# The first chunk's first layer in two halves of its contraction, one more weight piece split on TensorE and ScalarE, and a new order of the first steps

## The chip, the core and the metric

The kernel runs on one core of a Trainium2 chip. The metric is the device time of one execution in microseconds (us), lower is better. A core has five engines that each work through their own instructions in order and wait for each other through semaphores: TensorE (PE in the profile; its weight loads are listed apart as PEld), VectorE (DVE), ScalarE (ACT), GpSimd (POOL) and SyncE (SP), which here only issues DMAs.

## What is computed

Attention with a band of 16 keys to either side and one summary key and value per block of 32 (4 batches, 8 heads, 768 positions, 64 dimensions), and behind it a two-layer network with a GELU on the 3072 resulting rows of 512. Cut to what matters:

```
k_sum = k.reshape(B, H, nb, 32, D).max(axis=3)
v_sum = v.reshape(B, H, nb, 32, D).mean(axis=3)
scores_l = where(|i - j| < 16, scale * q @ k.T, -1e9)
scores_s = scale * q @ k_sum.T + log(32)
a = softmax(concat([scores_l, scores_s]))
x = (a @ concat([v, v_sum]))          # regrouped to (3072, 512)
h = x @ w_in                          # w_in: 512 x 2048
g = 0.5 * h * (1 + erf(h / sqrt(2)))
out = g @ w_out                       # w_out: 2048 x 512
```

All inputs are float32. TensorE takes float16 here, so a large product is made of three: each operand a is split into a high half (a rounded to float16) and a low half (the rest), and high x high, high x low and low x high are summed. A few early products are made in float32 instead.

## The kernel before

**Attention units.** The attention runs in 24 units of 4 heads x 256 positions; the first six lie in batch 0. Units 0 to 2 work in float32 (`f_scores`, `f_sums`, `f_values`), later ones with halves (`scores`, `sums`, `values`). A unit's path: `k_pack` (ACT packs keys and block maxima into `kf`), `f_mask` (PE writes the mask into PSUM), `f_scores` (PE), `evac` (ACT), `maximum` (POOL, a maximum over partitions), `m_shift` (PE subtracts it), `m_exponent` (ACT), `f_sums` and `f_values` (PE), `norm_take`, `norm_cross`, `norm_rec`, `norm_spread`, `norm_mult` (DVE, but `norm_cross` is ACT's), and `x_hi` (ACT) and `x_lo` (DVE), which leave the rows of x as two halves in `xos`. `f_values` needs the means of the summary values in its value tile; `s_load_vs` (ACT) or `load_vs` (POOL) copies them from the result of `sum_vt` (PE) and `mean_vt` (ACT).

**The network.** A chunk is 256 rows of x; chunk c takes units 2c and 2c+1, one for each half of the contraction over 512. `phase1 c i` multiplies it with piece i of `w_in` (8 pieces of 256 columns) in 24 products of 128x256: for each of two output halves e, four contraction blocks k, three products each. Blocks k = 0, 1 come from the first unit and k = 2, 3 from the second. `gelu`, `g_hi` (ACT) and `g_lo` (DVE) follow, and `phase2` multiplies with `w_out`. From chunk 4 on another scheme is used, which the change doesn't touch.

**Weights.** The weights arrive as 64-bit floats. `fetch_w_in` loads a piece, three DVE passes (`wi_bits i 0, 1, 2`) turn the bits into float32 in `wt`, `wi_hi` (ACT) makes the high half in `ww`, and the low half comes in one of two ways. `wi_lo` is one DVE pass. `wi_diff i h` and `wi_dlo i h` do half a piece each: PE takes wt minus the high half with a scaled identity (`eye`, float32) and its negative (`neg`, float16), and ACT writes the result as float16:

```
def wi_diff(i, h):
    ps = diffs["i", i, h] = ps_h.tile([P, 2, CH], F32, tag="psh", name=f"psw_{i}_{h}")
    ...
    nc.tensor.matmul(flat, eye, wt[:, i, h * 512 : (h + 1) * 512], start=True, stop=False)
    nc.tensor.matmul(flat, neg, w_part(i, 0, ks), start=False, stop=True)
...
def wi_dlo(i, h):
    ...
    nc.scalar.activation(w_part(i, 1, ks), flat.rearrange("p (r j) -> p r j", j=P), AF.Copy)
```

Before the change, piece 5 alone is done in the second way.

**Order.** `ORDER` is a table of 1936 steps. The program goes through it once, and each step appends its instructions to its engines, so the table sets the order on every engine and of the DMAs on SP's queue. `SLOTS` says which buffer each tile of a pool takes. Steps that start with `a_` issue their DMA from ACT's queue.

**Fills.** `fill n` is a step in which PE multiplies ones by ones into a PSUM tile that nobody reads: 3 products of 512 columns into `pso`, or 6 of 256 into `psd`. There are nine, and 16 such products of 512 columns at the very start (`pso_fill_s`). Each of the two PSUM pools has one buffer.

Of the kernel before, what the change touches and what calls it, by code (L numbers as in the profile page):

```python
# [84 lines left out]
wi_bits 4 2, wi_bits 5 0, sum_vt 1, evac 2, norm_take 0, wi_hi 4, wi_bits 5 1, fill 0, norm_cross 0, sum_vt 2, load_q
3, m_shift 1, s_q_hi 3, wi_bits 5 2, mean_vt, s_load_vs 0, maximum 2, m_shift 2, k_sums 0 0, fetch_w_in 2 2, norm_rec
0, load_v 1, f_values 0, norm_spread 0, wi_lo 4, fetch_w_in 3 3, q_lo 3, wi_bits 2 0, wi_bits 2 1, load_v 2, norm_mult
0, m_exponent 1, wi_bits 2 2, load_q 4, s_load_vs 1, load_k 4, x_hi 0, m_exponent 2, x_lo 0, f_sums 1, norm_take 1,
f_values 1, wi_bits 3 0, wi_bits 3 1, f_mask 3, norm_cross 1, scores 3, evac 3, wi_hi 5, fetch_w_in 1 1, fill 2,
load_v 4, norm_rec 1, norm_spread 1, wi_bits 3 2, norm_mult 1, s_k_hi 4, x_hi 1, fill 3, f_sums 2, norm_take 2,  # L90
load_vs 2, f_mask 4, wi_hi 3, s_q_hi 4, x_lo 1, norm_cross 2, k_lo 4, wi_diff 5 0, wi_dlo 5 0, wi_diff 5 1, f_values
2, phase1 0 4, maximum 3, fetch_k 1 3, load_v 3, wi_bits 1 0, load_vs 3, q_lo 4, wi_bits 1 1, shift 3, wi_bits 1 2,
phase1 0 0, wi_hi 2, load_vs 4, norm_rec 2, norm_spread 2, exponent 3, wi_dlo 5 1, wi_lo 3, phase1 0 5, wi_hi 1,
norm_mult 2, gelu 0 4, gelu 0 5, prep_k 1 3, wi_lo 2, fetch_w_in 6 2, f_sums 3, norm_take 3, x_hi 2, wi_lo 1, scores
4, load_k 5, wi_bits 6 0, fetch_k 1 0, norm_cross 3, f_values 3, norm_rec 3, x_lo 2, evac 4, maximum 4, fetch_w_in 7
3, norm_spread 3, prep_k 1 0, phase1 0 3, phase1 0 1, gelu 0 0, g_hi 0 4, norm_mult 3, load_q 5, wi_bits 6 1, s_q_hi
5, x_hi 3, q_lo 5, phase1 0 2, g_hi 0 0, fetch_w_out 0 4, fetch_w_out 1 5, gelu 0 3, fetch_k 2 1, x_lo 3, shift 4,
g_hi 0 5, wi_bits 6 2, s_k_hi 5, k_lo 5, g_lo 0 4, g_lo 0 5, exponent 4, wo_bits 0 0, gelu 0 1, phase1 1 4, f_values
4, wi_bits 7 0, g_lo 0 0, load_k 6, wo_bits 0 1, g_hi 0 3, gelu 0 2, s_k_hi 6, f_sums 4, norm_take 4, wo_bits 0 2,
gelu 1 4, wi_bits 7 1, load_q 6, load_v 5, wi_hi 6, phase1 1 3, g_hi 0 2, wo_bits 1 0, g_hi 0 1, g_lo 0 1, wo_hi 0,  # L100
phase1 1 1, norm_cross 4, wo_bits 1 1, wi_bits 7 2, fetch_w_out 2 4, phase1 1 0, wo_lo 0, g_hi 1 4, gelu 1 1, g_lo 0
3, wi_hi 7, fetch_k 1 1, f_mask 5, scores 5, evac 5, phase1 1 5, wo_bits 1 2, g_lo 1 4, wo_hi 1, wi_lo 7, gelu 1 3,
g_hi 1 1, wi_lo 6, s_q_hi 6, g_hi 1 3, q_lo 6, gelu 1 5, g_hi 1 5, wo_lo 1, g_lo 1 5, prep_k 1 1, f_mask 6, phase1 1
2, prep_k 2 1, gelu 1 2, fetch_w_out 3 5, maximum 5, phase1 0 7, phase1 0 6, wo_bits 2 0, g_lo 1 3, wo_bits 2 1,
norm_rec 4, norm_spread 4, wo_bits 2 2, g_lo 0 2, wo_bits 3 0, gelu 0 7, prep_k_end 1 0, wo_bits 3 1, gelu 1 0, phase1
1 6, k_sums 1 0, g_hi 1 0, load_v 6, g_hi 1 2, g_lo 1 1, wo_bits 3 2, phase2 0 1, gelu 0 6, g_lo 1 2, shift 5,
fetch_w_out 4 4, k_lo 6, wo_hi 3, load_q 7, wo_hi 2, wo_lo 2, exponent 5, wo_lo 3, g_hi 0 6, wo_bits 4 0, norm_mult 4,
phase2 0 0, s_q_hi 7, wo_bits 4 1, phase1 1 7, gelu 1 7, scores 6, load_vs 5, fetch_w_out 5 5, x_hi 4, wo_bits 5 0,
wo_bits 4 2, f_sums 5, f_values 5, wo_bits 5 1, norm_take 5, evac 6, phase2 0 2, wo_bits 5 2, f_mask 7, g_hi 0 7,
wo_hi 4, wo_lo 4, norm_cross 5, fetch_v 1 2, wo_hi 5, wo_lo 5, phase2 0 3, norm_rec 5, norm_spread 5, x_lo 4,  # L110
norm_mult 5, g_lo 1 0, maximum 6, load_v 7, x_hi 5, x_lo 5, q_lo 7, fetch_w_out 6 4, g_lo 0 7, phase2 0 5, g_hi 1 7,
shift 6, fetch_k 1 2, phase2 0 4, gelu 1 6, load_k 7, s_k_hi 7, wo_bits 6 0, phase1 2 6, gelu 2 6, exponent 6, k_lo 7,
fetch_w_out 7 5, prep_v 1 2, g_lo 0 6, g_lo 1 7, phase1 2 4, gelu 2 4, load_k 9, wo_bits 7 0, g_hi 1 6, prep_k 1 2,
prep_k_end 1 1, g_hi 2 4, g_lo 1 6, phase1 2 1, wo_bits 7 1, s_p_hi 6, wo_bits 6 1, wo_bits 7 2, phase1 2 0, gelu 2 1,
fetch_v 1 1, load_q 9, p_lo 6, gelu 2 0, fetch_v 1 0, load_mask, k_sums 1 1, wo_hi 7, s_q_hi 9, wo_bits 6 2, phase1 2
7, wo_hi 6, wo_lo 7, wo_lo 6, scores 7, s_k_hi 9, sums 6, fetch_v 1 3, prep_v 1 1, q_lo 9, prep_v 1 0, fetch_k 2 0,
fetch_v 2 1, prep_v 1 3, phase1 2 3, k_lo 9, fetch_k 2 3, load_vs 6, phase2 0 6, store 0 0, phase2 0 7, g_hi 2 1, g_lo
2 1, g_lo 2 4, norm_take 6, evac 7, load_q 8, prep_k 2 0, prep_v 2 1, phase2 1 0, g_hi 2 6, phase2 1 2, phase2 1 4,
gelu 2 3, gelu 2 7, prep_k 2 3, norm_cross 6, load_vs 7, v_hi 6, maximum 7, load_k 8, wt_add 1 0, g_hi 2 7, v_hi 7,
s_k_hi 8, wt_add 1 1, v_lo 6, fetch_v 2 2, shift 7, s_q_hi 8, v_lo 7, exponent 7, norm_rec 6, scores 9, values 6,  # L120
load_v 9, prep_k_end 2 0, phase2 1 6, k_lo 8, q_lo 8, norm_spread 6, load_k 11, g_hi 2 3, prep_v 2 2, add_mask 9,
s_p_hi 7, p_lo 7, load_q 11, maximum 9, norm_mult 6, wt_add 1 2, x_hi 6, phase1 2 5, g_lo 2 6, phase1 2 2, put 0 0,
wt_hi 1, store 1 0, s_q_hi 11, scores 8, x_lo 6, gelu 2 5, add_mask 8, load_v 8, sums 7, norm_take 7, load_vs 9,
norm_cross 7, put 1 0, wt_lo 1, g_lo 2 7, fetch_k 2 2, shift 9, s_k_hi 11, norm_rec 7, q_lo 11, maximum 8, gelu 2 2,
values 7, g_hi 2 2, v_hi 9, phase2 1 1, norm_spread 7, phase2 1 3, store 0 1, g_hi 2 5, norm_mult 7, k_lo 11, x_hi 7,
g_hi 2 0, g_lo 2 2, x_lo 7, phase2 1 5, shift 8, exponent 8, v_lo 9, phase1 3 2, prep_k 2 2, g_lo 2 5, s_p_hi 8,
phase2 1 7, load_q 10, p_lo 8, s_q_hi 10, wt_add 0 0, g_lo 2 0, load_vs 8, v_hi 8, exponent 9, load_k 10, fetch_v 2 0,
v_lo 8, load_v 11, phase1 3 4, s_k_hi 10, sums 8, g_lo 2 3, scores 11, add_mask 11, load_v 10, wt_add 0 1, values 8,
put 0 1, q_lo 10, wt_add 0 2, phase1 3 5, gelu 3 2, load_vs 10, k_lo 10, norm_take 8, s_p_hi 9, p_lo 9, phase1 3 6,
maximum 11, wt_hi 0, norm_cross 8, sums 9, scores 10, norm_rec 8, norm_spread 8, q_cast 12, load_k 12, gelu 3 6, store  # L130
1 1, norm_mult 8, gelu 3 5, prep_v 2 0, load_vs 11, x_hi 8, add_mask 10, v_hi 10, values 9, norm_take 9, wt_lo 0, ws
0, norm_cross 9, g_hi 3 6, put 1 1, shift 11, g_hi 3 2, gelu 3 4, x_lo 8, fetch_v 2 3, exponent 11, phase1 3 1,
norm_rec 9, norm_spread 9, s_p_hi 11, norm_mult 9, maximum 10, q_neg 12, v_hi 11, k_sums 2 0, phase1 3 7, v_lo 10,
phase2 2 1, g_lo 3 2, phase2 2 3, shift 10, phase1 3 0, wt_add 2 0, v_lo 11, load_v 12, exponent 10, g_hi 3 5, p_lo
# [1409 lines left out]
```

## Time and profile before

| | us |
|---|---|
| median of three runs | 560.56 |
| the three runs | 559.53, 560.56, 561.64 |
| the profiled execution: its own time | 559.72 |
| its span, from the first instruction to the last | 557.7 |
| busy in the span: PE / PEld | 551.1 / 415.9 |
| busy in the span: DVE / ACT / POOL | 480.2 / 387.8 / 110.8 |

An engine is busy while one of its instructions runs; with PE, products overlap, so its busy time says how long at least one was under way. The difference between the profiled execution's time and its span, 2.0 us, lies before the first and behind the last instruction.

### The profile page before, as it was taken

To read this page: it belongs to the slowest core of one execution; us is meant where nothing else is said; L and a number is where in the kernel's file an instruction comes from. 1 tells how busy PE (TensorE), PEld (TensorE's weight loads), DVE (VectorE), ACT (ScalarE), POOL (GpSimd) and SP (SyncE) were. 2 spreads that over 40 slices of the span, in tenths; PEclk is the share of its full clock that TensorE was granted. 3 is DMA by queue.
4 is the path that set the end of the run, shared out by engine and by line. 5 is a ranking of instruction groups with operands and counts; after the bars stand their busy time and mean duration, and the time that the engine had idled before them with its cause. 6 is when DMAs were issued, how large, how long until landed. Compare 5 with 4: busy or idle time off the path is not lost.

```text
span 557.7 us, 14490 instructions
## 1 busy us (share of the span) xinstructions
PE 551.1 (99%) x6161; PEld 415.9 (75%) x6161; DVE 480.2 (86%) x679; ACT 387.8 (70%) x678; POOL 110.8 (20%) x66
## 2 busy tenths in 40 slices
PE   8999999999999999999999999999999999999997
PEld 5558886685677566677765657888888888888886
DVE  5899999999989999999999989998887895384811
ACT  4698858568688988689887568686577765355610
POOL 2644030302415223163312202103220000000000
PEclk9999999999999999999999999999999999999999
DMA  8979535757455656636565442447954220000102
GB/s 327 398 278 396 212 126 177 263 145 208 157 168 171 138 140 192 141 53 179 138 155 154 151 123 81 104 138 197 286 177 148 61 94 1 1 1 29 48 1 86
DMA packets 42640, 84.26 MB, mean 151 GB/s; under 512 B 4176, under 2 KB 16720, under 8 KB 42064
## 3 DMA queue, kind: packets, MB, share of 16 engines
q1 hardware_dynamic: 38832, 79.85, 43.3%
q0 software_dynamic: 3456, 3.15, 5.1%
q8 instruction: 48, 0.79, 0.6%
q10 hardware_dynamic: 288, 0.34, 0.2%
q14 instruction: 16, 0.13, 0.1%
...
## 4 chain that ended last, share of the span: by engine, by line
PE 97%; ACT 1%; POOL 1%; issue 0%; POOLq 0%
PE psy L1105 15%; PE pso_y L1389 8%; PE pso L1153 8%; PE psz L1105 8%; PE pso L1154 7%; PE pso L1155 7%; PE psh L1034 5%; PE psh L1035 5%; PE psh L1036 5%; PE psx L1105 4%; PE psd_y L1389 4%; PE pss_x L1389 4%; PE pss L875 3%; PE psv L957 3%; PE psv_z L1389 2%; PE psn L973 1%
## 5 line engine op out<-in xcount | busy, mean ns | idle before, releaser
L904 POOL PARTITION_ALL_REDUCE m<-s x23 | 82.0, 3566 | 185.8 <-DVE w_out_l L589 40.8
L1105 PEld LDWEIGHTS <-wt 128*128 128x128 f16 x768 | 74.4, 98 | 10.1 <-issue 0.2
L1153 PE MATMUL pso<-w_out_h,gg 128*128 128x512 f16 x192 | 72.9, 380 | 0.0
L1154 PE MATMUL pso<-w_out_l,gg 128*128 128x512 f16 x192 | 72.8, 379 | 0.0
L1155 PE MATMUL pso<-w_out_h,gg 128*128 128x512 f16 x192 | 72.8, 379 | 0.0
L1105 PE MATMUL psy<-xos,wt 128*128 128x256 f16 x576 | 70.5, 273 | 0.0
L1034 PE MATMUL psh<-xos,ww 128*128 128x256 f16 x256 | 69.9, 273 | 0.0
L1036 PE MATMUL psh<-xos,ww 128*128 128x256 f16 x256 | 69.8, 273 | 0.0
L1035 PE MATMUL psh<-xos,ww 128*128 128x256 f16 x256 | 69.8, 273 | 0.0
L1105 PEld LDWEIGHTS <-ww 128*128 128x128 f16 x576 | 55.8, 98 | 8.9 <-issue 0.4
L1389 PEld LDWEIGHTS <-gg 128*128 128x128 f16 x576 | 55.9, 98 | 7.6 <-issue 1.1
L1116 ACT ACTIVATE ww<-psy 128x512 f32<-128x512 f32 x48 | 28.3, 591 | 27.4 <-PE psy L1105 27.3
L1155 PEld LDWEIGHTS <-gg 128*128 128x128 f16 x192 | 18.8, 98 | 22.7
L1153 PEld LDWEIGHTS <-gg 128*128 128x128 f16 x192 | 18.8, 98 | 19.8 <-issue 0.4
L1154 PEld LDWEIGHTS <-gg 128*128 128x128 f16 x192 | 18.8, 98 | 19.1
L1389 PEld LDWEIGHTS <-wt 128*128 128x128 f16 x288 | 28.1, 98 | 3.6 <-issue 0.4
L1232 DVE SCALAR_TENSOR_TENSOR gg<-h,gg 128x512 f16<-128x512 f32 x32 | 21.5, 686 | 10.1 <-ACT gg L1229 9.9
L1034 PEld LDWEIGHTS <-ww 128*128 128x128 f16 x256 | 25.0, 98 | 4.5 <-issue 0.8
L1035 PEld LDWEIGHTS <-ww 128*128 128x128 f16 x256 | 25.1, 98 | 3.5
L1036 PEld LDWEIGHTS <-ww 128*128 128x128 f16 x256 | 25.1, 98 | 2.9
L1043 ACT ACTIVATE g<-psh 128x512 f32<-128x512 f32 x32 | 19.0, 593 | 10.9 <-DVE gg L1052 6.7
L909 DVE TENSOR_TENSOR s<-s,m 128x1024 f32<-128x1024 f32 x21 | 25.6, 1217 | 0.1
(224 smaller groups left out, 1372.3 us busy)
## 6 DMA issues: line engine op xcount, KB each, us to landing
...
```

Source lines behind the costliest of these rows:

```text
L904: nc.gpsimd.partition_all_reduce(out_ap=self.m32, in_ap=self.s32, channels=P, reduce_op=bass_isa.ReduceOp.max)
L909: nc.vector.tensor_tensor(out=self.s32, in0=self.s32, in1=self.m32, op=ALU.subtract)
L1034: nc.tensor.matmul(ph[:, e, :], wh, xh, start=(k == 0), stop=False)
L1035: nc.tensor.matmul(ph[:, e, :], wh, xl, start=False, stop=False)
L1036: nc.tensor.matmul(ph[:, e, :], wl, xh, start=False, stop=(k == NCC - 1))
L1105: nc.tensor.matmul(ps[:, e, :], ws, xx, start=(first and e == 0 and k == 0 and m == 0), stop=(k == 1 and m == 2), skip_group_check=True,)
L1116: nc.scalar.activation(snaps[b, q, n], split8(acc[b, q, "y"]), AF.Copy)
L1153: nc.tensor.matmul(p, gh, w_out_h[:, f, :], start=(f == 0), stop=False)
L1154: nc.tensor.matmul(p, gh, w_out_l[:, f, :], start=False, stop=False)
L1155: nc.tensor.matmul(p, gl, w_out_h[:, f, :], start=False, stop=(f == NFC - 1))
L1232: nc.vector.scalar_tensor_tensor(out=a_part(b, q, m, 1), in0=h_src(b, q, m), scalar=SC_G, in1=a_part(b, q, m, 0), op0=ALU.mult, op1=ALU.su ...
L1389: nc.tensor.matmul(ps, g, ww_, start=(first and e == 0 and k == 0), stop=(e == 1 and k == 2), skip_group_check=True,)
```

## The change

`phase1` takes a third argument. Without it all 24 products are issued as before; with h = 0 or 1, only the 12 of one half of the contraction: h = 0 needs the first unit of the chunk alone, h = 1 the second. The two halves add up in the same PSUM tile, for which the first product of the tile alone now carries the start flag. All eight pieces of chunk 0 are issued in halves; for pieces 0 and 4 other steps stand between the two halves, for the other six the halves follow each other directly.

Piece 3's low half is no longer made by `wi_lo` but by `wi_diff 3 h` and `wi_dlo 3 h`, as piece 5's is.

The first 419 steps of `ORDER` become 430 in a new order; they are the same steps but for those two changes. The 1517 steps behind them are unchanged, and from there on each tile follows the same tile in its buffer as before. `SLOTS` is rewritten to go with it.

```diff
@@ ORDER (its first two lines; some 80 more are re-sorted)
-fill 10, a_load_m16, fetch_k 0 0, a_load_q 0, fill 8, fetch_w_in 0 0, prep_k 0 0, k_pack 0, prep_k_end 0 0, fill 1,
-f_mask 0, fetch_k 0 1, load_ind, f_scores 0, fetch_vt 0, fill 12, fetch_w_in 4 4, wi_bits 0 0, load_q 1, evac 0,
...
+a_load_q 0, fetch_k 0 0, prep_k 0 0, a_load_m16, fetch_w_in 0 0, fill 3, wi_bits 0 0, wi_bits 0 1, f_mask 0, fill 2,
+fetch_k 0 1, load_ind, wi_bits 0 2, k_pack 0, f_scores 0, k_pack 2, evac 0, fill 4, prep_k 0 1, fill 12, fetch_vt 0,
...
-    def phase1(c, i):
-        ph = pht[c, i] = ps_h.tile([P, 2, CH], F32, tag="psh", name=f"psh_{c}_{i}")
+    def phase1(c, i, h=None):
+        if not h:
+            pht[c, i] = ps_h.tile([P, 2, CH], F32, tag="psh", name=f"psh_{c}_{i}")
+        ph = pht[c, i]
+        ks = range(NCC) if h is None else range(2 * h, 2 * h + 2)
         for e in range(2):
-            for k in range(NCC):
+            for k in ks:
                 x = xo[2 * c + k // 2]
                 wh, wl = (ww[:, z, k, e, i, :] for z in range(2))
                 xh, xl = (x[:, z, k % 2, :] for z in range(2))
-                nc.tensor.matmul(ph[:, e, :], wh, xh, start=(k == 0), stop=False)
-                nc.tensor.matmul(ph[:, e, :], wh, xl, start=False, stop=False)
-                nc.tensor.matmul(ph[:, e, :], wl, xh, start=False, stop=(k == NCC - 1))
+                for m, (ws, xx) in enumerate(((wh, xh), (wh, xl), (wl, xh))):
+                    nc.tensor.matmul(
+                        ph[:, e, :], ws, xx, start=(e == 0 and k == 0 and m == 0),
+                        stop=(k == NCC - 1 and m == 2), skip_group_check=True,
+                    )
```

Three places show what the new order does. The first is PE's, from unit 0's scores (`pss_0`) to its `m_shift` (the row that reads `m32_0`); `psv_vt` is `sum_vt`, and each fill stands here with one row of its three or six. Before:

```order
L796 MATMUL pss_0_157<-q32_0_136,kf_0_147 128x64 x16
...
L442 MATMUL pso_fill_12_181<-ones_89 64x512
...
L442 MATMUL psd_fill_11_194<-ones_89 64x256
...
L651 MATMUL psv_vt_212<-w_out_h_97,w_out_l_98 88x512 x2
...
L764 MATMUL pss_1_0_215<-mask16_sb_88 128x2x64
...
L855 MATMUL pss_0_157<-m32_0_207,neg_1_87 128x512 x2
```

And of the change:

```order
L797 MATMUL pss_0_145<-q32_0_130,kf_0_157 128x64 x16
...
L443 MATMUL pso_fill_4_181<-ones_89 64x512
...
L443 MATMUL pso_fill_12_186<-ones_89 64x512
...
L765 MATMUL pss_1_0_201<-mask16_sb_88 128x2x64
...
L443 MATMUL psd_fill_11_217<-ones_89 64x256
...
L443 MATMUL psd_fill_0_224<-ones_89 64x256
...
L652 MATMUL psv_vt_231<-w_out_h_97,w_out_l_98 88x512 x2
...
L443 MATMUL psd_fill_8_234<-ones_89 64x256
...
L856 MATMUL pss_0_145<-m32_0_211,neg_1_87 128x512 x2
```

Unit 1's mask and two more fills have moved ahead of `m_shift`, one of them and the mask ahead of `sum_vt` too; ahead of the scores stand two fills in place of three.

The second place is PE's too, where the first layer begins. `psn` is `f_sums`, `psv_1` and `psv_2` are `f_values`, `psw` is `wi_diff`, `psh_0_4` is `phase1 0 4`; of 12 or 24 like products one row stands. Before:

```order
L818 MATMUL psn_2_476<-wt_94,ones_f_92 32x256 x4
...
L537 MATMUL psw_5_0_500<-wt_94,w_out_l_98 128x512
...
L537 MATMUL psw_5_1_504<-wt_94,w_out_l_98 128x512
...
L810 MATMUL psv_2_507<-wt_94,v32_2_356 64x64 x16
...
L1034 MATMUL psh_0_4_524<-xos_96,ww_93 128x256
...
L1034 MATMUL psh_0_0_562<-xos_96,ww_93 128x256
```

And of the change:

```order
L819 MATMUL psn_2_449<-wt_94,ones_f_92 32x256 x4
...
L1039 MATMUL psh_0_0_465<-xos_96,ww_93 128x256
...
L811 MATMUL psv_1_479<-s32_1_265,v32_1_351 64x64 x16
...
L1039 MATMUL psh_0_4_500<-xos_96,ww_93 128x256
...
L538 MATMUL psw_3_1_523<-wt_94,w_out_l_98 128x512
L539 LDWEIGHTS w_out_l_98
L539 MATMUL psw_3_1_523<-ww_93,w_out_l_98 128x512
L811 MATMUL psv_2_539<-wt_94,v32_2_375 64x64 x16
...
L538 MATMUL psw_3_0_558<-wt_94,w_out_l_98 128x512
```

The first halves of pieces 0 and 4 now stand ahead of the values of units 1 and 2, and piece 3's two differences between those; piece 5's have moved further ahead. Further on, and not shown here, the first product of the second layer (`phase2 0 0`) now stands behind eleven pieces of the first layer (six of chunk 0, five of chunk 1), where before it stood behind fifteen.

The third place is ACT's, from unit 2's `evac` (the row that writes `wt` from `pss_2`) to `s_load_vs 0` (the row that writes `v32_0`). `rc_0` is `norm_cross 0`, `qh_3` is `s_q_hi 3`, `w_out_h` from `psv_vt` is `mean_vt`, and `s32_1` from `pss_1` is `m_exponent 1`. Before:

```order
L891 ACTIVATE wt_94<-pss_2_246 128x1024
L526 ACTIVATE ww_93<-wt_94 128x8x128
L988 ACTIVATE rc_0_305<-dent_0_294 128x16
L993 ACTIVATE rc_0_305<-dent_0_294 32x8 x4
L829 ACTIVATE qh_3_317<-q32_3_313 128x512
L658 ACTIVATE w_out_h_97<-psv_vt_212 24x512
L723 ACTIVATE v32_0_283<-w_out_h_97 24x1024
```

And of the change:

```order
L892 ACTIVATE wt_94<-pss_2_279 128x1024
L989 ACTIVATE rc_0_304<-dent_0_299 128x16
L994 ACTIVATE rc_0_304<-dent_0_299 32x8 x4
L527 ACTIVATE ww_93<-wt_94 128x8x128 x2
L659 ACTIVATE w_out_h_97<-psv_vt_231 24x512
L863 ACTIVATE s32_1_265<-pss_1_0_201 128x512
L863 ACTIVATE s32_1_265<-pss_1_1_202 128x512
L724 ACTIVATE v32_0_322<-w_out_h_97 24x1024
```

`s_load_vs 0` now stands behind two `wi_hi` and behind `m_exponent 1`, and `s_q_hi 3` has moved behind it.

## Rows read from the trace of the kernel before

**Rows 1.** The page: PE's busy time, and the granted clock in 40 slices.
```profile
PE 551.1 (99%) x6161; PEld 415.9 (75%) x6161; DVE 480.2 (86%) x679; ACT 387.8 (70%) x678; POOL 110.8 (20%) x66
...
PEclk9999999999999999999999999999999999999999
```

**Rows 2.** Waits of PE: what for, total us, times, longest us.
```profile
PE pso_fill_s L442 <- POOL warm L454: 0.9, 1, 0.9
PE psv_vt L651 <- DMA w_out_h<-in_vt_dram: 0.7, 1, 0.7
PE pso_y L1389 <- ACT g_os L1411: 0.5, 1, 0.5
PE psv L810 <- ACT v L723: 0.5, 1, 0.5
PE pss L764 <- ACT wt L862: 0.4, 1, 0.4
PE pss L855 <- POOL m L904: 0.3, 1, 0.3
```

**Rows 3.** Windows: stretch, busy us (instructions) of PE, PEld, DVE, ACT, POOL.
```profile
40.00:60.00 20.00, 20.00 (x252) 17.46 (x249) 19.97 (x27) 16.63 (x29) 6.59 (x3) 1.00 0.81 309
...
400.00:500.00 100.00, 100.00 (x1087) 88.06 (x1086) 75.93 (x116) 64.60 (x124) 3.22 (x1) 1.00 0.25 80
```

**Rows 4.** Timeline of PE: start us, us, instruction, idle before it and its releaser.
```profile
0.94 5.07 PE L442 MATMUL pso_fill_s<-ones 128*64 128x512 f16 x16 [0.94 <-POOL warm L454]
6.07 0.81 PE L442 MATMUL pso_fill<-ones 128*64 128x512 f16 x3
6.72 0.82 PE L442 MATMUL psd_fill<-ones 128*64 128x256 f16 x6
...
8.65 2.00 PE L796 MATMUL pss<-q,kf 64*128 64x64 f32 x32
...
12.79 1.92 PE L651 MATMUL psv_vt<-w_out_h,w_out_l 128*88 128x512 f32 x4 [0.71 <-DMA w_out_h<-in_vt_dram]
14.55 0.60 PE L764 MATMUL pss<-mask_sb 128*128 128x128 f16 x4
...
28.45 1.15 PE L810 MATMUL psv<-s,v 128*64 128x64 f32 x32
...
36.65 1.08 PE L537 MATMUL psw<-wt,w_out_l 128*128 128x512 f32 x2
...
38.95 1.15 PE L810 MATMUL psv<-wt,v 128*64 128x64 f32 x32
...
40.15 0.27 PE L1035 MATMUL psh<-xos,ww 128*128 128x256 f16 x1
40.26 0.27 PE L1036 MATMUL psh<-xos,ww 128*128 128x256 f16 x1
...
49.37 1.15 PE L810 MATMUL psv<-s,v 128*64 128x64 f32 x32
```

**Rows 5.** Timeline of ACT, columns as in the timeline of PE.
```profile
7.53 0.42 ACT L783 ACTIVATE kf<-ks_f 128x256 f32<-128x256 f32 x1 [1.12 <-DVE ks_f L624]
...
22.11 1.02 ACT L891 ACTIVATE wt<-pss 128x1024 f32<-128x1024 f32 x1 [2.23 <-PE pss L796]
...
24.23 0.89 ACT L993 ACTIVATE rc<-dent 32x8 f32<-32x8 f32 x4
...
27.26 1.05 ACT L723 ACTIVATE v<-w_out_h 24x1024 f32<-24x1024 f32 x1
...
40.53 0.60 ACT L543 ACTIVATE ww<-psw 128x512 f16<-128x512 f32 x1
```

**Rows 6.** Timeline of POOL: unit 0's maximum.
```profile
11.82 3.53 POOL L904 PARTITION_ALL_REDUCE m<-s  x1 [9.83 <-ACT s L891]
```

**Rows 7.** Groups of DVE by form, first 45 us: count, busy us, mean ns, idle before.
```profile
L624 DVE TENSOR_REDUCE ks_f<-w_out_l 128x48 f32<-128x1536 f32 x2 | 3.5, 1748 | 5.7 <-DMA w_out_l<-in_kp_dram 5.7
...
L529 DVE SCALAR_TENSOR_TENSOR ww<-wt,ww 128x1024 f16<-128x1024 f32 x2 | 2.4, 1216 | 0.0
```

More of the change, by code (lines that the diff above doesn't have):

```diff
@@ L85 @@
[L85 to L134, printed above, removed]
@@ new lines @@
+wi_bits 5 2, k_lo 3, wi_hi 5, norm_rec 0, norm_spread 0, wi_lo 4, load_v 0, sum_vt 1, sum_vt 2, mean_vt, m_shift 1,
+fetch_w_in 3 3, m_exponent 1, s_load_vs 0, load_k 4, wi_diff 5 0, wi_dlo 5 0, wi_bits 2 0, maximum 2, fill 10, m_shift
+2, m_exponent 2, load_v 1, s_q_hi 3, wi_bits 2 1, wi_bits 2 2, f_values 0, norm_mult 0, load_v 2, fetch_k 1 3, f_sums
+1, f_mask 3, norm_take 1, q_lo 3, wi_diff 5 1, x_hi 0, scores 3, norm_cross 1, f_sums 2, wi_bits 3 0, s_load_vs 1,
+x_lo 0, load_vs 2, wi_hi 2, load_q 4, evac 3, k_sums 0 0, phase1 0 0 0, wi_dlo 5 1, f_values 1, wi_bits 3 1, maximum
@@ new lines @@
+gelu 2 3, s_k_hi 8, load_q 8, prep_v 2 1, v_lo 6, phase2 1 4, fetch_v 2 2, shift 7, s_q_hi 8, v_lo 7, exponent 7,
+norm_rec 6, scores 9, values 6, load_v 9, prep_k_end 2 0, phase2 1 6, k_lo 8, q_lo 8, norm_spread 6, load_k 11, g_hi 2
+3, prep_v 2 2, add_mask 9, s_p_hi 7, p_lo 7, load_q 11, maximum 9, norm_mult 6, wt_add 1 2, x_hi 6, phase1 2 5, g_lo 2
+6, phase1 2 2, put 0 0, wt_hi 1, store 1 0, s_q_hi 11, scores 8, x_lo 6, gelu 2 5, add_mask 8, load_v 8, sums 7,
+norm_take 7, load_vs 9, norm_cross 7, put 1 0, wt_lo 1, g_lo 2 7, fetch_k 2 2, shift 9, s_k_hi 11, norm_rec 7, q_lo
@@ new lines @@
+11, maximum 8, gelu 2 2, values 7, g_hi 2 2, v_hi 9, phase2 1 1, norm_spread 7, phase2 1 3, store 0 1, g_hi 2 5,
+norm_mult 7, k_lo 11, x_hi 7, g_hi 2 0, g_lo 2 2, x_lo 7, phase2 1 5, shift 8, exponent 8, v_lo 9, phase1 3 2, prep_k
+2 2, g_lo 2 5, s_p_hi 8, phase2 1 7, load_q 10, p_lo 8, s_q_hi 10, wt_add 0 0, g_lo 2 0, load_vs 8, v_hi 8, exponent
+9, load_k 10, fetch_v 2 0, v_lo 8, load_v 11, phase1 3 4, s_k_hi 10, sums 8, g_lo 2 3, scores 11, add_mask 11, load_v
+10, wt_add 0 1, values 8, put 0 1, q_lo 10, wt_add 0 2, phase1 3 5, gelu 3 2, load_vs 10, k_lo 10, norm_take 8, s_p_hi
@@ new lines @@
+9, p_lo 9, phase1 3 6, maximum 11, wt_hi 0, norm_cross 8, sums 9, scores 10, norm_rec 8, norm_spread 8, q_cast 12,
+load_k 12, gelu 3 6, store 1 1, norm_mult 8, gelu 3 5, prep_v 2 0, load_vs 11, x_hi 8, add_mask 10, v_hi 10, values 9,
+norm_take 9, wt_lo 0, ws 0, norm_cross 9, g_hi 3 6, put 1 1, shift 11, g_hi 3 2, gelu 3 4, x_lo 8, fetch_v 2 3,
+exponent 11, phase1 3 1, norm_rec 9, norm_spread 9, s_p_hi 11, norm_mult 9, maximum 10, q_neg 12, v_hi 11, k_sums 2 0,
+phase1 3 7, v_lo 10, phase2 2 1, g_lo 3 2, phase2 2 3, shift 10, phase1 3 0, wt_add 2 0, v_lo 11, load_v 12, exponent
@@ new lines @@
+10, g_hi 3 5, p_lo 11, g_lo 3 5, sums 11, values 11, phase2 2 5, s_k_hi 12, x_hi 9, prep_v 2 3, prep_k_end 2 1, gelu 3
+0, k_lo 12, wt_add 2 1, wt_add 3 0, q_cast 13, wt_add 2 2, k_sums 2 1, x_lo 9, norm_take 11, s_p_hi 10, p_lo 10,
+wt_add 3 1, q_acc 12, wt_hi 2, g_hi 3 0, scores 12, gelu 3 1, phase2 2 7, g_lo 3 6, g_lo 3 0, add_mask 12, q_neg 13,
+norm_cross 11, load_vs 12, v_hi 12, g_hi 3 4, norm_rec 11, load_k 13, wt_add 3 2, q_acc 13, norm_spread 11, maximum
+12, sums 10, norm_mult 11, s_k_hi 13, norm_take 10, store 2 1, phase1 3 3, norm_cross 10, gelu 3 3, k_lo 13, phase2 2
```

168 lines of the change are left out of this document (97 added, 71 removed).

## The prediction

> **What bounds the kernel now.** I read the page first, then PE's waits, then windows, then the timelines of the first 50 us. The page shows PE busy for 99% of the span and the granted clock at full in all forty slices [rows 1]. That alone proves little, since products overlap, so the second view counts: PE's waits add up to 3.3 us in the whole execution, and five of the six come before 33 us [rows 2]. The first, 0.9, is the start itself. The 0.5 on `pso_y` lies in the unchanged steps. What lies in the re-sorted steps and could go is 0.7 (the values for `sum_vt`), 0.3 (unit 0's maximum), 0.5 (`s_load_vs 1`) and 0.4 (a PSUM tile that `m_exponent 2` reads): 1.9 us. [...] So the time is PE's work plus what PE waits in the first 33 us, and a change can save no more than it takes from these two.
>
> The profiled execution took 559.72 us, 0.84 less than the median of 560.56; I add my difference to the median. The three runs differ by 2.1 us, so 0.5%, or 2.8 us, is about what can be told from no change.
>
> **The change part by part.**
>
> Piece 3's low half. PE gets two more pairs of products (float32 and float16). Piece 5's two pairs stand in one block, from 36.65 to 38.95 [rows 4]: **+2.3 us** of PE work. No other engine's work hides that, because PE is what everything waits for. DVE loses one pass of 1.2 us [rows 7], ACT gains two of 0.6 [rows 5].
>
> The halves. The same 24 products per piece, each 0.11 as before; only their place differs. The start flag costs nothing. Nothing to add, except that products of different kinds now alternate more often; the float32 pairs stand alone in four places instead of one, and PE needs a little to change kind. I take 0.1 for that, an estimate.
>
> The nine fills. All stay, each 0.65 (6.72 minus 6.07 [rows 4]). A fill right behind another in the same single buffer must wait for it: the first one starts at 6.07, after the starting products have ended at 6.01, whereas the next, in the other pool, starts 0.16 before its predecessor ends [rows 4]. So that succession costs 0.2. Before it happens once, now twice (12 behind 4, 0 behind 11): +0.2.
>
> The waits, one by one, by laying PE's new order end to end.
>
> First, `f_scores 0`. Only two fills stand ahead of it, and the first of them follows the starting products in the other pool, so PE is ready at 8.65 - 0.65 - 0.2 = 7.8. But `kf` is ready only at 7.95 [rows 5], so PE waits: **+0.2**, and the scores start at 8.0, 0.65 before the old 8.65. Unit 0's maximum, which ended at 11.82 + 3.53 [rows 6], ends at 14.7.
>
> Second, `sum_vt 0`. PE was ready at 12.79 - 0.71 = 12.1 [rows 4]. Now a fill (0.65) and unit 1's mask (0.6) more stand ahead, and the two 0.2 from above: 13.7, behind the data at 12.79. The wait of 0.7 is gone. The sum takes 14.55 - 12.79 = 1.76, `fill 8` 0.65: `m_shift 0` is issued at 16.2, behind the maximum at 14.7. The 0.3 is gone.
>
> Third, `f_values 0`. From `m_shift 0` to the end of `sum_vt 2` PE has one fill less than before, so a lag of 0.8 becomes 0.15. Then a half of piece 5's difference (1.15) and `fill 10` (0.65) stand ahead of `f_values 0`, which before started at 28.45 [rows 4]: now 30.4. What it needs last is `s_load_vs 0`. On ACT it started at 27.26 and took 1.05 [rows 5]; it now stands behind `m_exponent 1` too, which itself waits for a `m_shift 1` that comes right behind `sum_vt 2`. I put it from 28.9 to 29.95. ACT's earlier work doesn't delay it: `evac 2` from 22.9, `norm_cross 0` (0.9 and 0.2), two `wi_hi` of 1.05 end near 27.2, when `sum_vt 2` has just ended. So no wait, but a lead of only 0.4. `f_values 1` and unit 3's mask, which before waited 0.5 and 0.4, now come at 36.9 and 32.2, when `s_load_vs 1` (35.0) and `m_exponent 2` (31.5) are done. Both waits are gone.
>
> Fourth, the first halves. Unit 0's `x_lo` ends near 34.6, and PE comes to `phase1 0 0 0` at 35.5. Piece 3's first difference is due at 39.4, when `wi_hi 3` has just ended; the float32 product, which goes first, doesn't read that, and covers 0.9. `f_values 2` needs `load_vs 2`, done near 37, at 40.5.
>
> Sum: +2.3 - 1.9 + 0.2 + 0.2 + 0.1 = **+0.9 us**. The common point to check it is the end of `f_values 3`: before and now, the same fills, masks, sums and three pieces of the first layer stand ahead of it. It was at 49.37 + 1.15 = 50.5 [rows 4], and comes at 51.4, with two more differences done. Behind it I find no wait: 560.56 + 0.9 = **561.4 us**.
>
> Bounds. Below: all waits gone, no new ones and no dearer change of kind, 2.3 - 1.9 - 0.2 = +0.2, and if the pairs hide 0.4 of each other's changes, -0.2. Above: none of the old waits gone and the small ones added, +2.8.
>
> **The rivals.**
>
> *An even trade (B).* As bounded below: each wait closes fully and `kf` is ready in time because the queries now load first on ACT's queue. 560.4 to 560.9. For it: the leads are all positive. Against: `kf` at 7.95 hangs on DVE's maximum, not on the queries.
>
> *VectorE falls behind (C), slower.* The second layer now begins behind eleven pieces rather than fifteen. From 51.4, eight pieces (24 x 0.109 each) and four small steps bring PE there at 75.5, and its ninth product needs `g_lo 0 1` at 77.3. DVE has 80 instructions up to that: 28 passes of 1.2 us (34) and 52 shorter ones, 31 in sum by my reading of the same view, from 5.7 us on [rows 7], with about 6 us of waits: 76.4. The lead is 0.9, and DVE has no slack to catch up (19.97 of 20 us busy [rows 3]). Up to 0.9 late costs nothing; beyond, each us late is one of PE's. If DVE runs 5% slower than laid out here, 3.5 us late, PE waits 2.6 and the time is 564.1. It becomes slower by over 0.5% from about 2.8 us late. A smaller form is `s_load_vs 0` late by 1 us: 0.6 us of PE, 562.0.
>
> *VectorE, not PE, is the bound (D), faster.* DVE is 86% busy [rows 1] and full from 40 us on; if PE's products only seemed dense, the 1.2 us off DVE would be what counts and 559.4 the time. Against it stand the starts 0.11 apart [rows 4]: a product that waited for DVE would start later. [...]
>
> *The halves do nothing (E).* If PE waited for unit 1's x anyway, the early halves would gain nothing. In my walk the fills and unit 0's chain, not x, hold PE up before 33 us, so the halves only move products; that is within the forecast.
>
> **How the numbers follow.** The forecast (+0.4 to +1.8, a wait more or less) 0.60; B 0.18; C in its small form or with 1 to 2.5 us 0.12, in its large form 0.06; D 0.04. The forecast is the likeliest, 561.4. From 560.0 (B, less the scatter of a median, 0.4) to 563.4 (the old waits kept, +2.8) about 0.86 is held; D and C's large form and part of the middle are left out. Beyond 0.5%: C's large form and a tail of the middle, 0.09 slower; D's 1.2 us and everything else on that side is less than 2.8, so 0.02 faster; the same 0.89.
>
> **What would show it.** PE's waits of the changed kernel should have lost the 0.7, 0.3, 0.5 and 0.4 and hold 0.2 on unit 0's scores. PE's busy time should rise by about 2, `f_values 3` should end near 51.4, and windows from 60 to 200 us should show PE full. The forecast is wrong if PE shows a wait behind 60 us, on `gg` or `w_out_l` from DVE above all, or if `f_values 0` waits for ACT.

## The result: slower by 0.6%

The changed kernel takes 563.79 us (median of six runs, 562.49 to 565.32), the kernel before 560.42 (six runs, 559.53 to 561.64). The ratio is 1.006, with a 95% interval of 1.0046 to 1.0075: +3.4 us. The forecast of 561.4 and its range up to 563.4 are missed. The profiled execution took 563.55 us, its span is 561.7, 4.0 longer than before.

The page of the changed kernel, against [rows 1]:

```profile
PE 554.9 (99%) x6167; PEld 416.3 (74%) x6167; DVE 479.6 (85%) x678; ACT 388.9 (69%) x680; POOL 109.5 (19%) x66
```

PE's waits, against [rows 2]:

```profile
PE pso_fill_s L443 <- POOL warm L455: 0.9, 1, 0.9
PE pso L1159 <- ACT ot L1166: 0.9, 1, 0.9
PE psh L1039 <- ACT g L1049: 0.9, 2, 0.5
PE pso_y L1395 <- ACT g_os L1417: 0.5, 1, 0.5
PE pso_y L1395 <- DMA wt<-t_dram: 0.3, 1, 0.3
```

The four waits of the first 33 us (0.7, 0.5, 0.4, 0.3) are gone, as forecast. In their place stand three that before doesn't have: one of 0.9 and two in the sum of 0.9. PE's timeline shows where, against [rows 4]:

```profile
0.94 6.10 PE L443 MATMUL pso_fill_s<-ones 128*64 128x512 f16 x16 [0.94 <-POOL warm L455]
...
8.94 2.00 PE L797 MATMUL pss<-q,kf 64*128 64x64 f32 x32
...
50.92 1.15 PE L811 MATMUL psv<-s,v 128*64 128x64 f32 x32
...
71.40 1.80 PE L1039 MATMUL psh<-xos,ww 128*128 128x256 f16 x15 [0.44 <-ACT g L1049]
...
114.64 0.60 PE L1039 MATMUL psh<-xos,ww 128*128 128x256 f16 x4 [0.47 <-ACT g L1049]
...
152.04 0.38 PE L1159 MATMUL pso<-w_out_h,gg 128*128 128x512 f16 x1 [0.93 <-ACT ot L1166]
```

The difference can be laid out by common points. The 16 starting products took 6.10 against 5.07: 1.03, and not the change's (they take 5.02 to 6.44 over the profiles below, whichever kernel it is). `f_values 3` starts at 50.92 against 49.37, 1.55 later. Taking the start's 1.03 off whole would make the change look too cheap, since a longer start also covers waits that the kernel before has. The kernel before with two VectorE passes more (an experiment below) is the same program up to this point, and in its profile the start took 6.19, the wait of 0.7 for `sum_vt` is gone, and that for unit 0's maximum is 0.7 instead of 0.3:

```profile
50.19 1.15 PE L816 MATMUL psv<-s,v 128*64 128x64 f32 x32
```

Against this start the change has cost 50.92 - 50.19 = 0.73 by `f_values 3`, or 0.82 with the 0.09 by which the two starts still differ. A later common point is unit 11's maximum. In POOL's timeline of the kernel before, the first row is unit 7's maximum and the last unit 11's:

```profile
131.34 3.22 POOL L904 PARTITION_ALL_REDUCE m<-s  x1 [25.97 <-DVE ks L624]
...
170.00 3.22 POOL L904 PARTITION_ALL_REDUCE m<-s  x1 [14.63 <-DVE pl L924]
```

And in the changed kernel:

```profile
134.59 5.18 POOL L905 PARTITION_ALL_REDUCE m<-s  x1 [26.24 <-ACT rc L994]
...
173.80 3.22 POOL L905 PARTITION_ALL_REDUCE m<-s  x1 [14.06 <-DVE pl L925]
```

173.80 - 170.00 = 3.80, of which 1.55 are from before 51 us. The other 2.25 are the three waits, 0.44 + 0.47 + 0.93 = 1.84, and 0.41 that the list doesn't count: a product of 256 columns is under way for 0.27 us and the next usually starts 0.11 behind it [rows 4], so when one comes late, the first 0.16 of its lateness don't show as idle time. The last 0.2 of the span's 4.0 is the wait for `t_dram` near 396 us.

Each of the three is a PSUM tile that ACT frees late. ACT in the changed kernel:

```profile
68.39 1.06 ACT L587 ACTIVATE w_out_h<-wst 128x1024 f16<-128x1024 f32 x1 [1.72 <-DVE wst L501]
69.46 1.28 ACT L1049 ACT_TABLE_LOAD   x1
70.76 0.60 ACT L1049 ACTIVATE g<-psh 128x512 f32<-128x512 f32 x1
...
112.70 1.28 ACT L1049 ACT_TABLE_LOAD   x1 [1.05 <-DVE gg L1058]
114.00 0.60 ACT L1049 ACTIVATE g<-psh 128x512 f32<-128x512 f32 x1
...
150.45 1.06 ACT L566 ACTIVATE wt<-t 128x1024 f16<-128x1024 f32 x1 [1.26 <-DVE t L561]
151.41 0.58 ACT L1166 ACTIVATE ot<-pso 128x512 f32<-128x512 f32 x1
```

At 70 us `phase1 1 0` needs the tile that `gelu 1 5` reads. That `gelu` had its input at 68.34, when the last product of `phase1 1 5` ended, but on ACT it stands behind `wo_hi 0`, which waits 1.72 for DVE's third pass over that weight and starts at 68.39, and the 1.28 of a table load come only then. At 114 us `gelu 2 0`, whose end frees the tile for `phase1 2 6`, writes into the buffer that `g_lo 1 6` on DVE reads, waits 1.05 for it, and the table load comes behind that wait too. At 151 us `store 1 0` stands behind `wt_hi 1`, which waits for `wt_add 1 2`. In all three ACT stands idle for DVE, at the instruction that PE needs or ahead of it. DVE in the changed kernel:

```profile
67.14 1.21 DVE L501 SCALAR_TENSOR_TENSOR wst<-xos,wst 128x1024 int32<-128x1024 int32 x1
...
133.49 0.95 DVE L625 TENSOR_REDUCE ks<-kp 128x24 f32<-128x768 f32 x1
...
139.80 1.23 DVE L910 TENSOR_TENSOR s<-s,m 128x1024 f32<-128x1024 f32 x1 [3.12 <-POOL m L905]
```

For the third there is a cause further back: DVE idles 3.12 us for unit 7's maximum. That maximum writes into a buffer that last held a key tile, read by DVE at 133.49 (`prep_k 2 0`); in the new order that step stands behind `wt_add 1 1` and `g_lo 2 4`, so the maximum starts at 134.59 instead of 131.34. It also takes 5.18 us instead of 3.22, so 2.0 of the 5.2 us by which it ends later are its own length. The 1.97 us that `wt_add 1 2` takes here (from 148.45; the same pass takes 0.42 later on) are no cause of the third wait: it takes as long in the kernel before (from 143.93), which doesn't have that wait. By windows, against [rows 3], DVE is busy 3.5 us less at 120 to 140, 0.7 less at 40 to 60, and 1.2 less at 20 to 40, where it was busy 17.86 before:

```profile
120.00:140.00 20.00, 20.00 (x244) 11.22 (x236) 19.85 (x28) 14.27 (x24) 3.22 (x1) 1.00 0.71 198
```

```profile
20.00:40.00 20.00, 20.00 (x227) 10.70 (x226) 16.67 (x21) 16.32 (x30) 8.93 (x4) 1.00 0.82 295
40.00:60.00 20.00, 20.00 (x255) 15.70 (x254) 19.26 (x25) 16.67 (x32) 10.00 (x5) 1.00 0.85 313
...
120.00:140.00 20.00, 20.00 (x205) 11.93 (x206) 16.37 (x21) 13.05 (x22) 5.18 (x1) 1.00 0.56 163
```

The first row is the kernel before's, the other three are the changed kernel's.

### The profile page after: what moved, and what is told of

Its sections match the earlier page's. It is cut to its first block, busy times and chain, and to the rows that moved or that the text cites. A ratio compares the mean times of both kernels' runs of the same rounds, so it can differ in the third digit from the quotient of the medians.

```text
span 561.7 us, 14504 instructions
## 1 busy us (share of the span) xinstructions
PE 554.9 (99%) x6167; PEld 416.3 (74%) x6167; DVE 479.6 (85%) x678; ACT 388.9 (69%) x680; POOL 109.5 (19%) x66
## 4 chain that ended last, share of the span: by engine, by line
PE 83%; DVE 11%; DMA 3%; ACT 1%; issue 1%; SPq 0%; POOL 0%; DVEq 0%; ACTq 0%; POOLq 0%
PE psy L1111 15%; PE psz L1111 8%; PE pso_y L1395 7%; PE psh L1039 7%; PE pso L1159 6%; PE pso L1161 6%; PE pso L1160 6%; PE psx L1111 4%; PE psd_y L1395 4%; PE pss_x L1395 4%; PE pss L876 2%; PE psv L958 2%; PE psv_z L1395 2%; DVE gg L1058 2%; DVE wst L497 1%; PE pso_fill_s L443 1%
## 5 line engine op out<-in xcount | busy, mean ns | idle before, releaser
L905 POOL PARTITION_ALL_REDUCE m<-s x23 | 83.3, 3621 | 188.2 <-ACT s L892 39.8
L1039 PE MATMUL psh<-xos,ww 128*128 128x256 f16 x768 | 87.2, 273 | 0.9 <-ACT g L1049 0.9
L913 ACT ACTIVATE s<-s 128x1024 f32<-128x1024 f32 x21 | 22.2, 1055 | 5.7 <-DVE s L910 5.4
L1111 PE MATMUL psx<-xos,ww 128*128 128x256 f16 x192 | 23.6, 273 | 0.0
L1111 PE MATMUL psz<-xos,ww 128*128 128x256 f16 x192 | 23.6, 273 | 0.0
L1111 PE MATMUL psy<-xos,ww 128*128 128x256 f16 x192 | 23.6, 273 | 0.0
```

Source lines behind the costliest of these rows:

```text
L905: nc.gpsimd.partition_all_reduce(out_ap=self.m32, in_ap=self.s32, channels=P, reduce_op=bass_isa.ReduceOp.max)
L913: nc.scalar.activation(self.s32, self.s32, AF.Exp, scale=QKSCALE)
L1039: nc.tensor.matmul(ph[:, e, :], ws, xx, start=(e == 0 and k == 0 and m == 0), stop=(k == NCC - 1 and m == 2), skip_group_check=True,)
L1111: nc.tensor.matmul(ps[:, e, :], ws, xx, start=(first and e == 0 and k == 0 and m == 0), stop=(k == 1 and m == 2), skip_group_check=True,)
```

## The experiments

Theory A holds that TensorE's own work and order decide, as the prediction had it, and that the new waits are places in ScalarE's order. Theory B holds that VectorE sets the pace from about 50 to 160 us and TensorE only shows it as waits. Where a text names a further theory, it says itself what that one expects. The kernel before was timed beside each group: 560.68 for the first four runs, 560.35 for the next four, 560.45 for the next three and 560.76 for the last. The ratios are to these. The changed kernel itself was timed once, beside a kernel before of 560.42, so a difference from its 563.79 is known to about 1 us either way.

**Three moves on ScalarE and VectorE**, in the changed kernel:

```diff
-wo_hi 0
...
 gelu 1 5
+wo_hi 0
...
+g_hi 1 6
 exponent 6
+g_lo 1 6
 prep_v 1 2
...
-g_hi 1 6
-g_lo 1 6
...
+store 1 0
 wt_hi 1
-store 1 0
```

> The changed kernel with three steps moved on ScalarE: `wo_hi 0` behind `gelu 1 5`, `g_hi 1 6` ahead of `exponent 6` (and `g_lo 1 6` ahead of `prep_v 1 2`), `store 1 0` ahead of `wt_hi 1`. Theory A (three PSUM buffers come free late, because the ScalarE instruction that frees them stands behind one that waits for VectorE): the waits of 0.44, 0.47 and 0.93 us near 70.7, 113.9 and 150.9 us go, and the time falls by 2.0 us, from 563.8 to 561.8. Theory B (VectorE itself is late there, and ScalarE only hands it on): PE waits as long a little later, and the time stays within 0.7 us of 563.8. Theory C (what costs is the two added pairs of products and the slow start): the waits were cover for something else, and nothing changes.

562.66 us, ratio 1.0037 (1.0025 to 1.0049): 1.1 less than the changed kernel. The three waits are gone, but new ones have come at 158 and 159 us, where chunk 3's first layer reaches unit 7's half: 0.2 for `x_hi 7` (ACT) and 0.7 for `x_lo 7` (DVE). PE's waits there:

```profile
PE psh L1046 <- DVE xos L1022: 0.7, 1, 0.7
...
PE pss L804 <- ACT kf L791: 0.2, 1, 0.2
PE psh L1046 <- ACT xos L1019: 0.2, 1, 0.2
```

DVE still idles 3.12 us for unit 7's maximum, so unit 7 is late as before. ScalarE's order is a cause, then, and the maximum another. The start took 5.02 here, and unit 0's scores wait 0.2 for `kf`, as forecast; `f_values 3` starts at 50.08, 0.76 later than before's 49.37 at the same start.

**Piece 3's low half back on VectorE**, in the changed kernel:

```diff
-wi_diff 3 0, wi_diff 3 1, wi_dlo 3 0, wi_dlo 3 1
...
+wi_lo 3
 wi_bits 1 0
```

> The changed kernel with piece 3's low half made by `wi_lo 3` again, one VectorE pass ahead of `wi_bits 1 0`, and without its two differences. PE has 2.3 us less to do, VectorE 1.2 us more. Theory A: PE reaches the three waits earlier by up to 2.3 us while ScalarE and VectorE are no earlier, so these waits grow by most of it: 563.0, at best 562.5. Theory B: VectorE is later by 1.2, the time rises by up to 1 us: 564.5. Theory C: PE's work is what counts, 561.5.

564.89 us, ratio 1.0075 (1.0057 to 1.0092). TensorE has 2.3 us less to do, VectorE 1.2 more, and the time does not fall; it is 1.1 above the changed kernel, intervals overlapping. The work comes back as waits on PE, most of all for `x_lo` on DVE at 41 and 60 us:

```profile
PE psh L1045 <- DVE xos L1021: 3.0, 2, 1.9
```

At 41 us PE comes 2.3 us sooner to the product that reads unit 1's `x_lo`, which ends hardly sooner (42.51 against 42.88). At 60 us unit 3's `x_lo` ends at 62.54 against 60.80: in this order the pass of 1.2 us makes it 1.7 later. Why that is more than the length of the pass was not traced. Here B is right.

**The first layer undivided**, in the changed kernel, each piece where its second half stood:

```diff
-phase1 0 0 0
...
-phase1 0 0 1
+phase1 0 0
```

> The changed kernel with all eight pieces of chunk 0 in one go again, each at the place of its second half; the new order and piece 3's differences stay. Theory A: PE has no other work of its own in the place of the two first halves (2.6 us), and waits for the values of units 1 and 2 and for `wi_hi 3` instead: 1 to 2.5 us slower than the changed kernel, 564.8 to 566.3, with the waits between 35 and 42 us. The rival that the halves do nothing: 563.8, no wait there.

564.48 us, ratio 1.007 (1.0052 to 1.0088): +0.7, which these intervals don't tell from nothing. The trace does show that the early halves cover something: without them PE waits 1.8 at 37 us, where A expected a wait, though for a PSUM tile that `wi_dlo 5 1` frees and not for the values or `wi_hi 3`, and with PE later by that the two waits for `gelu` disappear.

```profile
PE psw L543 <- ACT ww L549: 1.8, 1, 1.8
```

**The changed kernel without fills 0 and 8**, 1.3 us of products that nobody reads.

> The changed kernel without `fill 0` and `fill 8` (1.3 us of products that nobody reads; the outputs don't depend on them). In the trace of the changed kernel PE waits for nothing between its start and 70 us. If PE's own work sets the pace up to there, everything behind the two fills comes 1.3 us earlier, and as ScalarE and VectorE follow PE there, the time falls by about 1.3, to 562.5. If VectorE sets the pace (theory B), PE gets new waits before 50 us or longer ones at 70.7, and the time stays within 0.5 of 563.8.

561.92 us, ratio 1.0026 (1.0016 to 1.0036): -1.9, which agrees with the 1.3 expected if PE's own work sets the pace. The trace is less clear, since it also has the signs named for B: a new wait of 0.2 for unit 0's maximum, one of 0.5 for unit 3's `x_lo` on DVE at 59 us, and at 70 us 0.7 in place of 0.44.

```profile
PE psh L1045 <- ACT g L1055: 0.9, 2, 0.7
...
PE psh L1045 <- DVE xos L1021: 0.5, 1, 0.5
PE pss L862 <- POOL m L911: 0.2, 1, 0.2
```

In this profile the start took 5.17, 0.93 less than in the changed kernel's, so with the fills' 1.3 PE was 2.23 ahead of the changed kernel at `m_shift 0`; at unit 11's maximum (172.50 against 173.80) 1.30 of that is left. One profile doesn't separate what the short start gave up from what the fills did. DVE, which in the changed kernel idles for PE at 21 and 33 us and for ACT at 26 and 57, gets its inputs earlier: it is busy 19.75 and 19.79 us in the windows 20 to 40 and 40 to 60, against 16.67 and 19.26.

**Unit 7's maximum in a buffer that comes free earlier**, in the changed kernel:

```diff
-fetch_k 2 3
+fetch_k 2 0
...
-prep_k 2 3
+prep_k 2 0
...
-fetch_k 2 0
+fetch_k 2 3
...
+prep_k 2 3
 wt_add 1 0
...
-prep_k 2 0
@@ SLOTS: from t32_1 on, buffers 2 and 3 of the pool exchanged
```

> The changed kernel with the fetches and reductions of the key tiles kp_2_0 and kp_2_3 exchanged, the buffers of unit 7's maximum and of t32_1 exchanged to fit, and the later reduction (now kp_2_3's) ahead of wt_add 1 0. Unit 7's maximum then takes a buffer whose last reader ends near 130.8 us, not 134.4. Theory B (VectorE sets the pace up to 160 us): the maximum starts near 131, VectorE's wait of 3.1 us for it goes, the 0.9 of PE at the store of chunk 1 goes, and the time is about 0.9 us below the changed kernel (563.8), near 562.9. Theory A (TensorE's own work decides and that wait is only one of ScalarE's order): the wait at the store stays and the time is within 0.3 of 563.8.

563.03 us, ratio 1.0045 (1.0029 to 1.0061): -0.8, as B had it, though this interval and the changed kernel's overlap. The trace tells more: the maximum starts at 131.70 and takes 3.22, DVE's idle 3.12 and PE's 0.9 at the store are gone; the two waits for `gelu` stay.

**The three moves and the early buffer together**, all nine fills kept.

> The changed kernel with the three moves and the early key tile together, all nine fills kept. This takes away the three new TensorE waits behind 50 us (0.5, 0.5, 0.9) and the VectorE wait of 3.1 us, and leaves the change's TensorE work as it is. If the prediction's sum was right and only those waits were overlooked: 561.4, the predicted time, or a little over (563.8 - 1.1 - 0.8 = 561.9 by adding the two runs). If VectorE's work itself is too much behind the later inputs, new waits of TensorE come up between 150 and 165 us and the time stays at 562.5 or above.

561.48 us, ratio 1.0014 (1.0001 to 1.0028). That is the predicted 561.4, closer than an interval of 560.5 to 562.0 can vouch for. PE's list holds nothing of the change any more but 0.2:

```profile
PE pso_y L1402 <- DMA wt<-t_dram: 1.2, 1, 1.2
PE pso_fill_s L450 <- POOL warm L462: 0.9, 1, 0.9
PE pso_y L1402 <- ACT g_os L1424: 0.5, 1, 0.5
PE pso L1168 <- DVE gg L1065: 0.2, 1, 0.2
```

So by the times the overlooked waits are worth 563.79 - 561.48 = 2.3 us, about 1 us either way. The two common points of the trace are here:

```profile
51.19 1.15 PE L818 MATMUL psv<-s,v 128*64 128x64 f32 x32
```

```profile
172.47 3.22 POOL L912 PARTITION_ALL_REDUCE m<-s  x1 [14.63 <-DVE pl L932]
```

They lie 121.28 us apart, against 122.88 in the changed kernel and 120.63 in the kernel before. By the trace, then, 1.60 of the 2.25 are regained. The other 0.65 are two short stops of PE for results of VectorE: for unit 3's `x_lo` at 61 us (0.14, too short for the list) and for `g_lo 0 1` at 78 us (the 0.2 in it), each with the 0.16 that don't show. VectorE's amount of work, the same as in the changed kernel, thus costs PE 0.65 us in this order.

**Those, and without fills 0 and 8.**

> The early key tile, the three moves of the first experiment and the two fills left out, all at once. If the three gains are separate (1.1, 1.9 and 0.9), the time is 563.8 - 3.9 = 559.9, a little under the kernel before (560.6). Theory B: with VectorE's wait for unit 7 gone the new wait of 0.7 at 157 us of the first experiment goes too, so 559.5 or less. If VectorE is simply full (its work, not its order), what one edit gives the next takes back, and the time stays at about 561.5.

560.14 us, ratio 0.9998 (0.9989 to 1.0008): 1.3 less again, the length of the two fills (0.9 by the ratios, whose intervals overlap a little). In the traces unit 11's maximum comes 1.90 earlier than in the run before, of which 0.28 are the start's. It is 3.6 us faster than the changed kernel and can't be told from the kernel before.

**The pairs for piece 3 alone, in the kernel before**:

```diff
 wi_diff 5 1
+wi_diff 3 0, wi_dlo 3 0
 f_values 2
+wi_diff 3 1, wi_dlo 3 1
 phase1 0 4
...
-wi_lo 3
```

> One part of the change alone, in the kernel before: the low half of piece 3 by two pairs of TensorE products and two ScalarE copies in place of one VectorE pass of 1.2 us; nothing else moves. Theory A (the prediction's term): TensorE's work decides, +2.3 us, near 562.9, with no new wait of TensorE. Theory B: VectorE sets the pace from 45 us on, so the pairs' 2.3 us are partly paid back by the pass of 1.2 us that VectorE saves: between -1 and +1 us, 559.6 to 561.6, and TensorE's gaps would show before 160 us where the kernel before has none only if VectorE is late.

562.33 us, ratio 1.0036 (1.0023 to 1.0048): +2.0 (1.3 to 2.7), against A's 2.3, with a new wait of 0.3. In the trace `f_values 3` starts 2.63 later than in the kernel before. The start is 0.35 longer, but the waits for `sum_vt` and unit 0's maximum are 0.3 shorter in sum, so that 2.6 are left: the pairs' 2.3 and the new wait. B's -1 to +1 falls: the pass of 1.2 us taken off VectorE brings nothing in this order.

**Two VectorE passes more, in the kernel before**:

```diff
 wi_bits 6 1
+wi_bits 6 1
...
 wi_bits 7 1
+wi_bits 7 1
```

> The kernel before with two VectorE passes of 1.2 us repeated (the second step of pieces 6 and 7, which changes nothing in the data): 2.4 us more on VectorE near 60 to 70 us, nothing else. Theory B: VectorE has no slack, TensorE waits for the 2.4 us at PSUM tiles that come free late: +2 us or more, near 562.8. Theory A: VectorE has a lead of some 1 us over TensorE and what is beyond it is caught up with in its later idle times: at most +1.4, and +0.3 if the lead is larger than I think.

562.68 us, ratio 1.0042 (1.0029 to 1.0056): +2.4 (1.6 to 3.1) for 2.4 us of VectorE. It appears on PE as waits for tiles that `gelu` frees, at 63, 73 and 88 us:

```profile
PE psh L1040 <- ACT g L1049: 1.3, 2, 0.8
...
PE pso L1159 <- ACT g L1049: 0.3, 1, 0.3
```

So neither A nor B holds alone. TensorE shows no gap from 40 to 200 us in the kernel before, and yet VectorE has little lead over what TensorE needs of it: 2.4 - 1.6 = 0.8 us by the listed waits, and less by common points. `f_values 3` was 0.82 later than in the kernel before, and unit 11's maximum is 2.95 later, so 2.1 of the 2.4 us reached PE and the lead was 0.3:

```profile
172.95 3.22 POOL L910 PARTITION_ALL_REDUCE m<-s  x1 [14.63 <-DVE pl L930]
```

**Six fills out**, with the moves and the early buffer: fills 1, 2, 10 and 12 too.

> The kernel with the moves, the early tile and fills 0 and 8 left out (560.1), without fills 1, 2, 10 and 12 as well: 2.6 us less of TensorE's work in the first 30 us. If TensorE's work alone sets the time there: 557.5. If VectorE, which has at most some 2 us of idle time left between 20 and 160 us, is right behind: no more than 1 us is gained, 559.1 to 560.1, and TensorE shows the rest as waits, some of them at the scores and masks of the first 30 us, where the maximum on GpSimd ends last, some between 50 and 120 us at tiles that gelu frees.

560.5 us, ratio 0.9994 (0.9983 to 1.0005). 2.6 us less work than the run with two fills out, and nothing gained. In this profile the start was also 0.75 shorter than in that run's (5.33 against 6.08), which brings PE sooner to what it then waits for. The first 30 us have other ends: the values' tile (1.2), unit 0's maximum (0.7), `kf` (0.7), the transfer for `sum_vt` (0.3); and behind them `x_lo` at 59 us:

```profile
PE psv L817 <- ACT v L730: 1.2, 1, 1.2
...
PE pss L862 <- POOL m L911: 0.7, 1, 0.7
PE psh L1045 <- DVE xos L1021: 0.7, 1, 0.7
PE pss L803 <- ACT kf L790: 0.7, 1, 0.7
```

**The same with two VectorE passes fewer.**

> As the run with six fills left out, and two VectorE passes of 1.2 us fewer: the second step of the pieces 6 and 7 is left out, so their weights lack the sign and the top bit of the exponent. If VectorE is right behind TensorE in that run, its waits behind 60 us go and the time falls by 1 us or more below that run. If something else (GpSimd's maxima, the first transfers) holds TensorE up there, the two runs agree within 0.4 us.

560.07 us, ratio 0.999 (0.9979 to 1.0002): -0.4 against the run before, at the edge of what its expectation calls agreement. The 0.7 for `x_lo` is gone, the first four are not. Those rather than VectorE hold TensorE up once the fills are out, as far as two intervals of 0.6 us either way can tell.

**The kernel before without fills 2 and 3.**

> The kernel before without fills 2 and 3, which stand from 34.09 to 35.6 us behind unit 3's scores: 1.3 us less of TensorE's work at a place where TensorE waits for nothing. If TensorE's work alone sets the time of the kernel before: 560.5 - 1.3 = 559.2. If VectorE follows closely behind (two added passes of 2.4 us came back as 1.7 us of TensorE's waits, so its lead is about 0.7 us): at most 0.7 is gained, 559.8 or a little above, and TensorE shows waits of some 0.6 us between 60 and 80 us at tiles that gelu frees, as with the two added passes. If the 1.9 us of the run without fills 0 and 8 was a gain that only the new order has, nothing is gained here.

560.67 us, ratio 0.9994 (0.9981 to 1.0008): nothing gained, and not by the mechanism that I expected. PE runs into unit 3's `evac` (0.5, at 35 us) and into `wi_dlo 5 1` (1.4, at 45 us), which on ACT stands behind `exponent 3`:

```profile
PE psh L1040 <- ACT ww L549: 1.4, 1, 1.4
...
PE pss L770 <- ACT s L897: 0.5, 1, 0.5
```

No version here beats the kernel before by more than these measurements can tell.

## Why the prediction was wrong

The step that failed is "Behind it I find no wait", the last of the sum. It stood for 0 and was 2.3 us: 2.25 in the changed kernel's trace, and by the times 563.79 with the three waits, 561.48 without them and with all else of the change in place. Behind `f_values 3` I had laid out one place only, `phase2 0 0` and its `g_lo 0 1`, and that one shows no wait. I had not asked of each PSUM tile behind 50 us what stands ahead, on ScalarE, of the instruction that frees it, nor what the moved `prep_k 2 0` releases, though the changed order shows both. The sign that the prediction names for being wrong, a wait of PE behind 60 us, came, but for ACT's `gelu` and `store`, not for `gg` or `w_out_l` from DVE.

The rest of the sum held. The pairs: +2.3 forecast, 2.0 (1.3 to 2.7) measured alone. The four waits: all gone. `f_values 3`: 0.9 later forecast, 0.76 measured between two short starts and 0.82 between two long ones. `kf`: 0.2, seen where the start was short; in the changed kernel's own profile the start's extra 1.03 hides it. The 0.1 for a change of kind is about what the traces show where products of another shape follow: from the first layer's last product to the values the starts lie 0.20 apart instead of 0.11. Between the float32 and float16 products of a pair they show nothing (0.43 and 0.22, as without a change), and the term was not measured alone. The start flag: nothing, as forecast; in the kernel before the products that carry it start 0.11 behind the one ahead of them, as the others do. PE's busy time rose by 3.8 where about 2 were forecast; 1.03 of it are the longer start. The whole: +0.9 forecast, +0.8 (0.1 to 1.6) once the overlooked waits are out; that the two medians meet to a tenth is luck.

Of the rivals, C comes nearest: VectorE late behind 50 us, 564.1 named, 563.8 measured. That the numbers come so close is luck. Its place was wrong, if not by much: `g_lo 0 1` ended at 77.77 and the product that reads it started at 78.31, without a wait. Its mechanism was only half right: in the changed kernel TensorE waits for no result of VectorE, but for ScalarE, which waits for VectorE ahead of work that is ready. Nor does VectorE's amount of work alone decide, since the reordered run has the same work and 0.65 us of stops in place of 2.25. My chance for C's large form was 0.06, and the range was cut below it. D falls: the pass off VectorE alone brings nothing that the runs can tell (2.0 for 2.3), and the 0.11 us from one start to the next in the first layer is half of the 0.22 that products of 512 columns take in the same trace. B's even trade falls with the result. On E, the halves alone can't be told from nothing; the 1.8 us wait in the undivided run says that they cover something.

"DVE loses one pass of 1.2 us" was worth nothing in the kernel before, as priced, but in the new order putting it back cost all of the 2.3 us of TensorE work that it saved. The price of a pass depends on what stands behind it.

What stays open: why fills 0 and 8 gave 1.9 in the changed kernel and 1.3 in the reordered one (the intervals overlap, and their profiles have starts of different length), and whether a better place for `wi_lo 3` would make the version without pairs the faster one.
